# Pooled scores and their products in single PSUM banks in the first eight pairs of an attention and gated-MLP kernel, with a new written-out order

## The chip, the cores and the metric

The kernel runs on one core of one Trainium2 chip. The metric is device time in microseconds (us) for one execution, lower is better. The engines are TensorE (PE; PEld is its weight load), VectorE (DVE), ScalarE (ACT), GpSimd (POOL) and the DMA queues, of which SyncE (SP) issues most.

## The reference

Inputs are q, k, v of shape (8, 8, 576, 64): batch, heads, sequence, head width. Attention has two parts that are added: one over pooled positions (means of four) with full softmax, its rows repeated four times, and a local one in which a position sees only positions less than four away. Its output, heads side by side, goes through a gated MLP.

```python
def sm_attn(qq, kk, vv):
    s = scale * np.matmul(qq, kk.transpose(0, 1, 3, 2))
    a = np.exp(s - np.max(s, axis=-1, keepdims=True))
    return np.matmul(a / (np.sum(a, axis=-1, keepdims=True) + 1e-09), vv)
out_up = np.repeat(sm_attn(q_d, k_d, v_d), 4, axis=2)      # q_d, k_d, v_d: means over groups of 4
scores = np.where(mask, scale * q @ k.T, -1e9)             # mask: |i - j| < 4
x = out_up + softmax(scores) @ v                           # (8, 576, 512)
h = np.maximum(x @ w_in, 0.0)                              # (8, 576, 1024)
u, w = h[..., :512], h[..., 512:]
w_n = (w - mean(w)) / np.sqrt(var(w) + 1e-06)              # over the last axis
w_s = np.einsum('ts,bsd->btd', w_spatial, w_n) + b_spatial[None, :, None]
out = (u * w_s) @ w_out                                    # (8, 576, 512)
```

The host only lays the inputs out; w_in and w_out arrive as 64-bit numbers and are decoded on the chip.

## The kernel before

Work is cut into batches (8), each of four pairs of heads (32 pairs, n = 0 to 31), and each batch then goes through the MLP.

**A pair** (function `attention`). q and k are loaded (qk). Sums over four positions (L720, L723) give the pooled k and q (kd). Local scores S go into a buffer ps by ten windows of 64 positions (L748); where the list ON["mask"] has T, two matmuls ahead of them (L741) add the mask in TensorE, else VectorE adds it (L761). Greatest (L770), difference (L776), exp (L791, or L788 on ScalarE where ON["sub"] has A), sum (L794), reciprocal (L797 and L801 on VectorE, L797 and L799 on GpSimd), division by it (L836), transpose T (L844) with its copy (L846). The pooled scores Sd (L810) make three parts of 144 columns: parts 0 and 2 in a buffer pd, part 1 in a buffer pe. Their greatest (L852 for parts 0 and 2 together, L853 for part 1, L854), exp with sums (L858), reciprocal (L862 with L866 or L864), normalising (L873 on ScalarE, L876 elsewhere), transposes Td (L891, two banks) with copies (L894), and products with the pooled v, AVd (L919, two banks' width), that are moved to dn by ScalarE (L923) and added by VectorE (L926). The local products AV (L952) are added to dn (L971, L973) and split in two f16 parts, x (L1002, L1004).

**A batch's MLP** (function `gated`). Products with the right half of w_in (V, L1029, first batch from 72 us on), their statistics and the split into f16 parts vh (L1038 to L1063), products with the left half (U, L1092), spatial products (SP, L1124), gate (L1145), and output products (O, L1160). The weights are decoded and split ahead of that on VectorE and ScalarE (L513, L539 to L547, L648).

**PSUM** has eight banks. Two double buffers, tag pa (paa, pab: two banks each), and four single ones, tag pm (pma to pmd). A pair from n = 8 on (MERGE = 8) keeps pooled scores and pooled products in the unused ends of the double buffers of local scores and products; in the first eight pairs each has a double buffer of its own. So such a pair takes five pa in turn (ps, pd, pt for T, one for AVd, one for AV) and three pm (pe, two for Td). The MLP's products take one pm each, as do the small products that find scales (L479, L486).

**Order.** The program builds a list of operations with engine, estimated duration and a rank (tables RANK, MRANK, WRANK plus EVICT), and `Plan.run` writes out the order greedily: on each engine, of the operations that could start within NEAR of the first, the lowest rank goes. A buffer is taken when an operation is placed. The lists ON say by index (pair n, or piece of the MLP for vlo) which engine does it; the last letter holds for all further indices. Operations marked port are kept from overlapping between VectorE and GpSimd by the estimate. Up to 110 us the planner fills gaps of TensorE with matmuls that compute nothing (L1204), where a single bank is free by its estimate.

Of the kernel before, what the change touches and what calls it, by code (L numbers as in the profile page):

```python
# [76 lines left out]
class Plan:  # L77
# [61 lines left out]
    def run(self, near=150.0, stay=0.0, dma=(1900.0, 900.0), emit=True):  # L139
# [110 lines left out]

RANK = {"load": [143.005, 47.751, 252.982, -69.47, -172.22, -274.786, 560.411, -758.364, -311.459, 313.434, 266.06, 380.575,
            943.336, 399.915],
        "vload": [391.404, 86.345, 272.249, 337.531, 429.684, -52.69, -370.895, -252.053],
        "vabs": [509.637, -1181.093, -217.316, 87.185, -457.776, 123.004, -794.489, 144.366],
        "tv": [-183.93, 240.18, 765.617, 930.011, 56.071, -19.127, -157.242, 125.859],
        "sum": [-115.268, 142.997, -94.455, -372.167, 362.55, -75.596, 306.456, 702.576, 1696.966, 425.169, -234.075, 705.288,
            -421.357, 223.437],
        "S": [-1061.927, -157.575, 379.809, -830.223, -915.099, 670.631, 141.564, -649.896, 467.386, 88.454, 513.148, 238.256,  # L260
            245.41, 202.772],
        "E": [-534.894, -339.729, -702.236, 21.188, 160.003, 471.872, 219.972, 899.326, -409.142, -823.461, -265.585, -479.069,
            -503.017, -440.633],
        "N": [231.109, -483.572, -754.504, 524.152, -141.085, 397.308, 1325.226, -80.846, -320.013, -220.077, -64.133, -498.673,
            700.859, -253.394],
        "T": [-347.227, -440.539, -1149.413, -139.403, 917.828, -1374.545, -1166.794, 234.909, 536.972, -105.532, -561.257,
            -49.343, -383.904, -24.157],
        "Sd": [-228.884, 341.247, -989.571, 12.731, -290.563, 65.584, -210.501, 584.996, 760.783, -156.288, -493.755, 182.161,
            -206.462, -81.893],
        "Nd": [20.186, -634.328, -625.655, -47.029, -1024.698, 6.919, -369.885, -166.975, -196.395, -51.441, 745.233, 26.68,  # L270
            590.548, 680.939],
        "Td": [226.557, -226.969, 765.057, -163.935, 412.294, -360.224, 842.794, -998.859, 11.321, 28.445, -152.942, 58.045,
            -1153.807, -259.463],
        "AVd": [377.528, -777.682, -319.581, 176.718, 599.105, 1049.442, -339.489, -191.118, -286.676, -150.229, -415.778,
            -182.501, -118.84, 141.634],
        "AV": [60.151, -170.544, -717.724, 720.142, -836.725, 275.504, 440.562, -339.226, -949.724, 57.757, -184.347, -239.42,
            -4.966, -560.047],
        "X": [49.462, -601.369, 382.04, -619.469, -420.239, 803.995, 16.415, -27.426, 201.671, 266.124, -288.114, 118.52,
            -424.608, -87.751]}
MRANK = {"V": [[-120.813, 103.137], [-373.166, -785.223], [-588.287, 86.439], [-457.053, -295.554], [-271.069, 53.075],  # L280
            [-161.929, 7.172], [-384.75, 67.584], [1.753, -86.54]],
        "U0": [[-381.018, 507.475], [-225.844, -398.15], [392.079, 353.99], [415.277, -261.891], [-69.09, -16.703], [-362.251,
            -497.795], [59.314, -190.411], [573.297, -308.684]],
        "S0": [[631.14, 127.639], [-206.013, -184.383], [299.174, 561.899], [-372.357, 30.262], [381.875, 239.103], [33.324,
            19.169], [-136.587, -125.569], [104.744, -531.737]],
        "U1": [[66.951, 205.966], [432.921, 80.243], [202.58, -320.842], [-584.875, -261.385], [85.111, -539.421], [-290.079,
            -515.53], [-73.151, -407.568], [-105.893, -362.577]],
        "O0": [[170.632, -34.982], [-172.469, 696.573], [159.95, -390.053], [-841.668, -359.026], [22.932, -667.87], [-349.956,
            231.605], [321.827, -73.48], [-54.093, -578.395]],
        "S1": [[-122.247, -1002.997], [272.521, 179.124], [-502.627, -34.942], [83.425, -28.324], [193.115, 251.294], [212.725,  # L290
            -514.576], [-0.655, 14.458], [254.101, -410.908]],
        "O1": [[-425.021, 297.386], [239.962, 469.652], [56.568, -208.235], [-194.872, 129.628], [-641.125, -6.104], [281.584,
            274.929], [184.644, 89.516], [19.298, 376.248]]}
EVICT = 456.633
WRANK = {"WV load": [31.22, -21.921, 242.309, 4.474],
        "WV decode": [350.543, -287.444, -567.367, 661.466],
        "WV bound": [-83.736, 162.235, 909.503, 36.755, -835.361],
        "WV split": [-201.598, 11.031, -341.826, -1007.43],
        "WU load": [-364.293, 427.826, 390.089, -59.831],
        "WU decode": [387.574, -316.232, 1019.795, 459.568],  # L300
        "WU bound": [1425.684, -228.293, 245.85, 118.051, 725.352],
        "WU split": [-187.848, -607.313, -258.771, -328.661],
        "WSP load": [289.708, -579.107, 622.627, -316.354, 744.76],
        "WSP bound": [397.382, 106.669, -930.598, 200.751, 873.332, -382.338],
        "WSP split": [-150.625, -91.686, 309.424, 430.824, -1165.74],
        "WO load": [201.774, -325.888, 429.457, 987.307],
        "WO decode": [137.835, 619.019, -225.889, -8.083],
        "WO bound": [-64.148, 457.463, -289.1, 18.247, -58.582],
        "WO split": [620.04, -563.746, 894.059, 1022.164]}
# [20 lines left out]


@with_exitstack
def tile_kernel(ctx, tc, qk, vw, v4, w_in, wT, bsp, w_out, out, emit=True):
# [365 lines left out]
    def attention(n):  # L699
# [550 lines left out]
```

## Time and profile before

| | |
|---|---|
| median of 3 runs | 579.53 us (578.91 to 579.99) |
| profiled execution | 580.97 us, span 579.1 us |
| mean granted TensorE clock | 0.995 of full |
| busy: PE, DVE, ACT, POOL | 551.6, 414.1, 376.3, 186.7 us |

Busy time is a sum over the instructions of an engine without overlap. "Granted clock" is the share of TensorE's full clock. An engine's idle time matters only where work that sets the end waits behind it.

### The profile page before, as it was taken

What the parts mean: (1) busy time and instruction counts of PE and PEld (TensorE: products, weight loads), DVE (VectorE), ACT (ScalarE), POOL (GpSimd) and SP (SyncE); (2) the same over time, 40 slices, a digit from 0 to 9 for tenths busy, and PEclk for the clock granted to TensorE, in tenths of its full rate; (3) what the DMA queues carried; (4) which work ended last, traced back from release to release, by engine and by line L of the source; (5) the groups of instructions that cost most, each with busy time, mean ns of one, the idle gap of its engine ahead of it and who ended that gap; (6) DMA issues with size and microseconds to landing.
All of it is one profiled execution on the core that took longest, in us unless ns stands there. A gap on an engine that the chain in (4) does not pass through costs nothing.

```text
span 579.1 us, 16048 instructions
## 1 busy us (share of the span) xinstructions
PE 551.6 (95%) x6501; PEld 368.0 (64%) x6501; DVE 414.1 (72%) x1084; ACT 376.3 (65%) x1076; POOL 186.7 (32%) x213
## 2 busy tenths in 40 slices
PE   5877899999999998999999999999999999999996
PEld 2445547764786566765776747778567567756752
DVE  5989899964898888578687776781976666844420
ACT  3689999457577677567575877565756665954422
POOL 3636533023531254154330432422422352202100
PEclk9999999999999999999999999999999999999999
DMA  8987870035322344225303343214220400010012
GB/s 285 338 241 213 215 180 1 1 102 143 88 83 91 115 103 126 65 90 138 86 20 119 99 113 102 84 65 108 77 100 2 138 2 19 8 32 1 20 54 74
DMA packets 37390, 57.04 MB, mean 99 GB/s; under 512 B 3650, under 2 KB 24130, under 8 KB 37316
## 3 DMA queue, kind: packets, MB, share of 16 engines
q1 hardware_dynamic: 35012, 48.94, 26.7%
q0 software_dynamic: 2304, 7.08, 7.2%
q8 instruction: 51, 0.84, 0.6%
q14 instruction: 23, 0.19, 0.1%
HBM read 46.57 MB, written 9.44 MB: 97 GB/s over the span
## 4 chain that ended last, share of the span: by engine, by line
PE 70%; DVE 18%; ACT 6%; issue 2%; DMA 2%; POOL 0%; SPq 0%; ACTq 0%; DVEq 0%; POOLq 0%
PE pmd L1124 4%; PE pma L1124 4%; PE pmb L1160 4%; PE pma L1160 4%; PE pmc L1029 4%; PE pmc L1160 4%; PE pma L1029 4%; PE pmc L1124 3%; PE pmb L1124 3%; PE pmd L1029 3%; PE pmd L1092 2%; PE pma L1092 2%; PE pmc L1092 2%; PE pmb L1029 2%; PE pmd L1160 2%
## 5 line engine op out<-in xcount | busy, mean ns | idle before, releaser
L1092 PEld LDWEIGHTS <-win 128*128 128x128 f16 x768 | 74.7, 98 | 20.8 <-issue 0.6
L1124 PEld LDWEIGHTS <-vha 128*128 128x128 f16 x768 | 74.0, 98 | 20.6 <-issue 2.1
L1160 PEld LDWEIGHTS <-gb 128*128 128x128 f16 x264 | 25.6, 98 | 28.5 <-issue 0.4
L1124 PE MATMUL pma<-wsp,vha 128*128 128x256 f16 (+1 forms) x216 | 29.4, 286 | 0.0
L1124 PE MATMUL pmd<-wsp,vha 128*128 128x256 f16 (+1 forms) x204 | 27.6, 285 | 1.3 <-DVE aua L1105 1.3
L1204 PE MATMUL pma<-mask_b,mask_a 128*128 128x512 bf16 x83 | 23.4, 415 | 3.1 <-DVE mask_a L383 3.1
L1124 PE MATMUL pmb<-wsp,vha 128*128 128x256 f16 (+1 forms) x180 | 24.1, 283 | 0.0
L1124 PE MATMUL pmc<-wsp,vha 128*128 128x320 f16 (+1 forms) x168 | 23.5, 290 | 0.0
L1160 PE MATMUL pmb<-wo,gb 128*128 128x512 f16 x96 | 22.0, 379 | 0.0
L1160 PEld LDWEIGHTS <-ga 128*128 128x128 f16 x120 | 11.6, 98 | 12.8 <-issue 0.2
L1057 POOL TENSOR_TENSOR sta<-sta,mhalf 128x1 f32<-128x1 f32 (+1 forms) x14 | 9.0, 646 | 32.3 <-DVE sta L1041 32.3
L669 POOL DMA_DIRECT2D tvb<-v_dram x12 | 10.8, 900 | 18.2 <-DMA tvb<-v_dram 15.7
L1160 PE MATMUL pma<-wo,gb 128*128 128x512 f16 x72 | 16.5, 379 | 0.0
L1029 PEld LDWEIGHTS <-xa 128*128 128x128 f16 x96 | 9.2, 98 | 10.8 <-issue 0.2
L1204 PEld LDWEIGHTS <-mask_a 128*128 128x128 bf16 x85 | 7.9, 104 | 12.6 <-issue 3.7
L720 POOL TENSOR_TENSOR suma<-qka 128x576 f32<-128x576 f32 x6 | 7.8, 1294 | 23.4 <-DMA qka<-qk_dram 23.4
L669 POOL DMA_DIRECT2D tva<-v_dram x12 | 10.8, 902 | 13.2 <-DMA tva<-v_dram 8.9
L1057 POOL TENSOR_TENSOR stb<-stb,mhalf 128x1 f32<-128x1 f32 (+1 forms) x15 | 10.9, 725 | 11.4 <-DVE stb L1041 11.4
L1160 PE MATMUL pmc<-wo,gb 128*128 128x512 f16 x60 | 13.8, 379 | 0.0
L1057 POOL TENSOR_TENSOR stc<-stc,mhalf 128x1 f32<-128x1 f32 (+1 forms) x11 | 7.5, 678 | 18.7 <-DVE stc L1041 15.2
L720 POOL TENSOR_TENSOR sumb<-qkb 128x576 f32<-128x576 f32 x6 | 7.8, 1296 | 16.5 <-DMA qkb<-qk_dram 16.5
L862 POOL TENSOR_SCALAR smdb<-smdb 112x3 f32<-112x3 f32 x3 | 0.6, 201 | 38.6 <-ACT eda L858 38.6
(1085 smaller groups left out, 1725.7 us busy)
## 6 DMA issues: line engine op xcount, KB each, us to landing
qka<-qk_dram SPq DMA_DIRECT2D x15, 576.0 KB, 4.9
qkb<-qk_dram SPq DMA_DIRECT2D x15, 576.0 KB, 6.2
tva<-v_dram POOLq DMA_DIRECT2D x12, 288.0 KB, 5.5
tvb<-v_dram POOLq DMA_DIRECT2D x12, 288.0 KB, 4.3
stg<-w_in_dram SPq DMA_DIRECT2D x5, 512.0 KB, 8.3
out_dram<-rowc SPq DMA_DIRECT2D x7, 256.0 KB, 2.2
out_dram<-rowb SPq DMA_DIRECT2D x7, 256.0 KB, 2.0
out_dram<-rowe SPq DMA_DIRECT2D x7, 256.0 KB, 2.1
```

What stands on the lines that cost most here:

```text
L669: plan.op("POOL", 850, lambda r=r: nc.gpsimd.dma_start(t.ap[LOW:KEYS], v4[b, r], accum_op=ALU.add), w=[t], rank=rank + 2.0 + 0.3 * r, kb=2 ...
L720: side(s1).tensor_tensor(sb.ap.rearrange("p x (g r) -> p x g r", r=2), x[:, :, :, :2], x[:, :, :, 2:], op=ALU.add)
L862: side(ivd).tensor_scalar(smd.ap[:PD], smd.ap[:PD], 1.0e-9, 4.0, op0=ALU.add, op1=ALU.mult)
L1029: nc.tensor.matmul(ps.ap, xs[c].ap[:, i, t * P:(t + 1) * P], win[:, c, j, FF:], start=(c == 0 and (i, j) == (0, 0)), stop=(c == NC - 1 and ...
L1057: plan.op("POOL", 530, lambda: nc.gpsimd.tensor_tensor(st.ap[:r, 8:9], st.ap[:r, 8:9], mhalf[:r], op=ALU.pow), w=[st], rank=rank - EVICT, ...
L1092: nc.tensor.matmul(ps.ap[:, :n], win[:, c, i, ft * P:(ft + 1) * P], xs[c].ap[:, j, HA[h]:HA[h + 1]], start=(c == 0 and (i, j) == (0, 0)), ...
L1124: nc.tensor.matmul(ps.ap[:, :n], vh.ap[:, c, i, fs], wsp[:, c, j, hs], start=(c == 0 and (i, j) == (0, 0)), stop=False)
L1160: nc.tensor.matmul(ps.ap, g.ap[:, c, HA[1] * i + k:HA[1] * i + k + P], wo[:, c, j, :], start=(c == 0 and (i, j) == (0, 0)), stop=(c == NF ...
L1204: nc.tensor.matmul(ap.rearrange("p (j k) -> p j k", k=64), mask_a, mask_b[:, None, :].broadcast_to([P, 8, 64]), start=True, stop=True)
```

## The change

For n < SMALL = 8 the pooled scores' parts 0 and 2 go to two single banks instead of one double buffer, and so do the pooled products (their local products keep a double buffer). A pair then takes three pa and seven pm. The greatest of parts 0 and 2 is found by two reduces instead of one. All ranks, EVICT, NEAR, STAY and the lists ON are new.

```diff
+SMALL = 8
-ON = {"sub": "DDDDDDADDADAAADDDADDAAADDDA",
-        "inv": "DDDDDPDDPDDPDPPDPDPDDPDPDDDPPPPD",
-        "invd": "DDDPDPPDDPDDDDDDPPDDPPDDDDPPPPD",
-        "sum": "DPPPDPPPDDPDPPDDDDPPDPDDDDPDDDPD",
-        "mask": "TTTTTTTTD",
-        "norm": "PDPPPDPDPPDDDPDPPPDPDPDPPPPDDPD",
-        "normd": "PAAPPDPPAAADDPAAPAPADAAPPPPADDAP",
-        "vlo": "PDPDPPPDDPDPDPDDDDPDDPPDDDPDPDDPDPDPDPD"}
+ON = {"sub": "DDDDDDADDADDDDADAAAAAADDAAAAAAD",
+        "inv": "DDDDDDDDDPDDDDDDDDPDPDPPPPDPPPD",
+        "invd": "DDDPDDPPDPDPDDDDPDDDDPPPPDPPPDP",
+        "sum": "DPPPDPDPDDDDPDPPPPDDPDDPPDDDDDP",
+        "mask": "TTTTTTTDTD",
+        "norm": "PDPDDDPPPPDPDPDPDDDPDDDPDPDDDDDP",
+        "normd": "PAAAPADADDAAAPDPPDAPDADPDAPDDDAD",
+        "vlo": "DDPDPDDDPPPPDDDPDPDDDDDPDDPDPD"}
...
-        merge = n >= MERGE
+        merge, small = n >= MERGE, n < SMALL
...
         def third(e):
-            return pe.ap[:, :G] if e == 1 else pd.ap[:, 256 * e + at:256 * e + at + G]
+            if e == 1:
+                return pe.ap[:, :G]
+            return pd[e // 2].ap[:, :G] if small else pd.ap[:, 256 * e + at:256 * e + at + G]
...
-            pd = plan.buf("pa")
+            pd = (plan.buf("pm"), plan.buf("pm")) if small else plan.buf("pa")
...
         def maximum_d():
-            nc.vector.tensor_reduce(mxd.ap[:PD, ::2], pd.ap[:PD].rearrange("p (e k) -> p e k", e=2)[:, :, at:at + G], axis=AX.X, op=ALU.max, negate=True)
+            if small:
+                for e in (0, 2):
+                    nc.vector.tensor_reduce(mxd.ap[:PD, e:e + 1], third(e)[:PD], axis=AX.X, op=ALU.max, negate=True)
+            else:
+                nc.vector.tensor_reduce(mxd.ap[:PD, ::2], pd.ap[:PD].rearrange("p (e k) -> p e k", e=2)[:, :, at:at + G], axis=AX.X, op=ALU.max, negate=True)
...
+        pdl = pdt if small else (pdt,)
         if not merge:
-            plan.op("PE", 610, scores_d, r=[kb], w=[pd, pe], hold=[ed], rank=R["Sd"], lag=PEL, mode="Q", name="Sd")
-        plan.op("DVE", 780, maximum_d, r=[pdt, pe], w=[mxd], rank=R["Sd"] - EVICT, port=True, name="maxd")
+            plan.op("PE", 610, scores_d, r=[kb], w=[*pdl, pe], hold=[ed], rank=R["Sd"], lag=PEL, mode="Q", name="Sd")
+        plan.op("DVE", 840 if small else 780, maximum_d, r=[*pdl, pe], w=[mxd], rank=R["Sd"] - EVICT, port=True, name="maxd")
...
-        if up:
+        if small:
+            two_w, two_v = (plan.buf("pm"), plan.buf("pm")), (plan.buf("pa"),)
+        elif up:
```

## Rows read from the trace of the kernel before

**Rows 1.** Busy time of each engine by stretch (microseconds from the start of the span; first the length of the stretch, then each engine's busy time with its number of instructions, the granted clock of TensorE, the share of DMA time and GB/s), and the sum over the whole span.
```profile
14.50:72.40 57.90, 46.31 (x775) 28.27 (x773) 52.44 (x134) 48.78 (x142) 31.10 (x33) 0.98 0.88 252
72.40:116.00 43.60, 41.88 (x339) 28.29 (x338) 42.11 (x119) 34.39 (x84) 11.04 (x12) 1.00 0.25 60
116.00:565.00 449.00, 446.26 (x5251) 303.54 (x5250) 310.89 (x814) 285.26 (x840) 139.52 (x149) 1.00 0.27 77
sum 579.10, PE 551.61 PEld 367.99 DVE 414.05 ACT 376.32 POOL 186.68; mean PE 110.32 PEld 73.60 DVE 82.81 ACT 75.26 POOL 37.34
```

**Rows 2.** The same table for the filler matmuls (line L1204) alone, opening stretch.
```profile
14.50:72.40 57.90, 18.55 (x70) 5.92 (x68) 0.98 0.88 252
```

**Rows 3.** The same table for all instructions, the last two quarters of the opening.
```profile
43.50:58.00 14.50, 11.34 (x243) 7.57 (x241) 14.30 (x34) 13.94 (x41) 9.16 (x10) 1.00 0.73 212
58.00:72.40 14.40, 11.92 (x241) 7.95 (x241) 12.75 (x39) 14.02 (x41) 8.47 (x9) 1.00 0.87 215
```

**Rows 4.** Waits of VectorE from 14.5 to 72.4 us: what waited, the releaser, microseconds in total, times, the longest.
```profile
DVE mxb L770 <- PE pab L748: 1.6, 1, 1.6
DVE mxc L770 <- PE paa L748: 0.6, 1, 0.6
DVE xfb L971 <- issue: 0.4, 1, 0.4
```

**Rows 5.** Waits of TensorE's matmuls in the same stretch, columns as in rows 4.
```profile
PE paa L952 <- ACT eda L858: 1.3, 1, 1.3
PE pab L952 <- ACT eda L858: 1.3, 1, 1.3
PE pab L741 <- DVE dnb L926: 1.2, 1, 1.2
PE paa L741 <- DVE sma L794: 0.9, 1, 0.9
PE paa L810 <- ACT edb L858: 0.6, 1, 0.6
```

**Rows 6.** From the timeline: VectorE and ScalarE instructions whose durations serve as prices (start, duration, engine, line, operation, output and inputs, count; in brackets the idle time before it and its releaser).
```profile
10.46 0.46 DVE L723 TENSOR_TENSOR kda<-suma 128x288 f32<-128x288 f32 x1
16.64 0.46 DVE L852 TENSOR_REDUCE mxda<-paa 112x2 f32<-112x288 f32 x1 [0.56 <-PE paa L810]
17.02 0.30 DVE L853 TENSOR_REDUCE mxda<-pmb 112x1 f32<-112x144 f32 x1
22.48 0.22 DVE L801 RECIPROCAL smb<-smb 128x10 f32<-128x10 f32 x1
24.06 0.81 DVE L836 TENSOR_TENSOR sb<-sb,smb 128x640 f32<-128x640 f32 x1
33.06 1.03 ACT L873 ACTIVATE eda<-eda,smdc 112x144 f32<-112x144 f32 x3 [0.51 <-DVE smdc L866]
```

**Rows 7.** From the timeline: matmuls and the ScalarE reads that end the use of the buffers with pooled scores of pair 0 (paa) and pair 7 (paa with pmc), in order of time.
```profile
17.36 0.47 PE L810 MATMUL pab<-kdb 64*64 64x144 f32 x8
18.79 0.38 ACT L858 ACTIVATE eda<-paa,mxda 112x144 f32<-112x144 f32 x1
19.31 0.43 PE L741 MATMUL paa<-mask_b,mask_a 128*128 128x320 bf16 x2 [0.90 <-DVE sma L794]
72.42 0.82 PE L1029 MATMUL pmb<-win,xa 128*128 128x512 f16 x3
75.02 0.81 PE L1029 MATMUL pma<-win,xa 128*128 128x512 f16 x3
76.17 0.38 ACT L858 ACTIVATE edb<-paa,mxdd 112x144 f32<-112x144 f32 x1
```

**Rows 8.** Four lines of code by instruction: count, duration in ns as least, median and greatest, first and last start in microseconds, shape.
```profile
L720 DVE TENSOR_TENSOR suma<-qka x9: 739/751/2402, 9.7 to 409.3; 128x576 f32<-128x576 f32 x9
L797 DVE TENSOR_SCALAR sma<-sma x5: 145/164/1020, 25.6 to 503.4; 128x10 f32<-128x10 f32 x5
L854 DVE TENSOR_SCALAR mxda<-mxda x8: 170/170/1173, 17.4 to 455.2; 112x3 f32<-112x3 f32 x8
L542 DVE TENSOR_SCALAR mba<-rowa x2: 428/956/1484, 6.5 to 50.4; 128x512 int32<-128x512 int32 x2
```

**Rows 9.** From the timeline: GpSimd instructions of the opening, columns as in rows 6.
```profile
27.45 1.14 POOL L720 TENSOR_TENSOR sumb<-qkb 128x576 f32<-128x576 f32 x1
43.91 0.91 POOL L876 TENSOR_TENSOR edb<-edb,smdd 112x432 f32<-112x432 f32 x1
44.78 1.26 POOL L836 TENSOR_TENSOR sa<-sa,smd 128x640 f32<-128x640 f32 x1
49.77 1.79 POOL L836 TENSOR_TENSOR sb<-sb,smb 128x640 f32<-128x640 f32 x1 [0.51 <-DVE smb L801]
55.84 0.89 POOL L864 TENSOR_TENSOR smda<-smda,minus 112x3 f32<-112x3 f32 x1
56.71 1.14 POOL L720 TENSOR_TENSOR suma<-qka 128x576 f32<-128x576 f32 x1
57.92 0.92 POOL L723 TENSOR_TENSOR kda<-suma 128x288 f32<-128x288 f32 x1
64.22 0.91 POOL L876 TENSOR_TENSOR eda<-eda,smdc 112x432 f32<-112x432 f32 x1
65.90 1.98 POOL L799 TENSOR_TENSOR smc<-smc,minus 128x10 f32<-128x10 f32 x1
```

More of the change, by code (lines that the diff above doesn't have):

```diff
@@ L247, in run @@
         return end
[L253 to L309, printed above, removed]
@@ L310 @@
-NEAR = 104.496
-STAY = 26.882
+RANK = {"load": [264.533, 33.649, 403.06, 186.653, -42.381, -410.839, 819.039, -607.622, -501.728, 243.085, 352.102, 354.132,
+            1093.505, 273.573],
+        "vload": [558.967, 276.5, 334.545, 308.567, 267.188, -101.291, -379.396, -222.862],
+        "vabs": [634.178, -1182.863, -145.804, -180.742, -589.109, 166.874, -730.049, 207.057],
+        "tv": [-43.519, 464.187, 742.381, 810.054, 111.484, -44.852, -198.988, 180.839],
+        "sum": [-322.043, 168.123, 112.107, -348.8, 434.587, 59.773, 244.669, 938.335, 1550.758, 527.842, -255.301, 697.748,
+            -232.674, 238.406],
+        "S": [-1302.427, 29.544, 240.133, -921.679, -943.4, 626.644, -32.63, -685.185, 661.359, 184.729, 567.017, 361.726,
+            321.012, 376.66],
+        "E": [-459.669, -527.995, -658.247, 159.782, 193.317, 620.643, 306.329, 873.564, -326.981, -885.141, -348.277, -551.906,
+            -474.543, -373.478],
+        "N": [285.362, -589.13, -711.842, 524.689, -161.908, 293.474, 1265.404, -30.543, -412.846, -159.808, -52.343, -537.504,
+            815.595, -307.896],
+        "T": [127.389, -609.648, -1127.039, -425.66, 749.486, -1310.231, -1100.363, 438.252, 691.047, -87.719, -528.186, -24.871,
+            -375.456, -91.404],
+        "Sd": [-347.5, 377.51, -1003.842, -215.136, -365.115, 138.976, -92.298, 652.174, 329.267, -160.095, -401.819, 232.758,
+            -236.92, -140.505],
+        "Nd": [238.956, -699.96, -990.36, -323.516, -1004.45, -222.865, -239.071, 39.976, -46.443, -133.498, 796.176, 63.19,
+            573.005, 754.815],
+        "Td": [354.384, -309.784, 945.407, -253.79, 312.905, -196.204, 736.782, -793.133, -122.62, 50.663, -245.263, 4.127,
+            -993.967, -317.459],
+        "AVd": [537.656, -772.178, -275.255, 18.365, 579.22, 945.875, -136.534, -217.582, -170.692, -264.39, -400.831, -116.318,
+            -79.309, -14.534],
+        "AV": [58.38, 226.865, -858.713, 622.045, -1014.049, 531.897, 160.75, -457.568, -982.583, 5.951, -166.95, -376.233,
+            -23.789, -699.464],
+        "X": [84.426, -678.614, 198.865, -615.758, -322.875, 1205.879, 53.938, -269.106, 245.79, 341.802, -225.41, 243.327,
+            -310.041, -131.769]}
@@ new lines @@
+MRANK = {"V": [[-357.918, 142.233], [-583.398, -902.948], [-392.849, 65.793], [-486.121, -186.54], [-280.761, 71.703], [-130.958,
+            80.968], [-507.617, 17.881], [65.81, -197.574]],
+        "U0": [[-349.34, 320.11], [66.062, -306.805], [332.204, 335.878], [316.833, -270.829], [-105.368, -214.951], [-323.961,
+            -452.914], [36.997, -107.838], [626.35, -336.686]],
+        "S0": [[493.25, -41.501], [-259.464, -183.334], [281.386, 638.165], [-394.019, 42.503], [488.16, 84.052], [92.242,
+            95.678], [-89.856, -104.179], [126.907, -592.501]],
+        "U1": [[12.184, 237.505], [257.792, -21.302], [159.007, -287.556], [-621.089, -364.793], [143.193, -392.905], [-338.506,
+            -488.257], [-13.595, -342.975], [-108.576, -404.447]],
+        "O0": [[225.164, 130.003], [-178.642, 778.718], [87.794, -329.345], [-911.542, -274.843], [133.598, -636.006], [-412.8,
+            235.349], [471.326, -78.114], [-117.512, -536.116]],
+        "S1": [[-2.809, -401.391], [302.578, 113.58], [-558.903, 129.581], [129.33, -158.619], [319.352, 256.614], [164.414,
+            -533.905], [-70.901, 129.294], [234.596, -407.925]],
+        "O1": [[-467.107, 369.251], [188.194, 415.668], [-56.45, -278.037], [-170.601, 91.132], [-852.743, 37.137], [186.673,
+            294.551], [295.701, 77.537], [10.665, 429.525]]}
@@ new lines @@
+EVICT = 412.459
+WRANK = {"WV load": [117.529, -191.416, 536.853, -123.356],
+        "WV decode": [381.441, -309.174, -504.673, 989.236],
+        "WV bound": [-96.239, 347.932, 921.213, 220.458, -744.06],
+        "WV split": [-41.433, 205.029, -31.901, -1111.787],
+        "WU load": [-505.686, 267.048, 436.293, -55.911],
+        "WU decode": [590.144, -496.64, 1133.635, 346.647],
+        "WU bound": [1437.453, -178.104, 204.387, 241.312, 794.104],
+        "WU split": [-340.217, -481.128, -248.193, -257.007],
+        "WSP load": [412.862, -748.696, 636.427, -698.741, 707.973],
+        "WSP bound": [338.999, 65.666, -1274.432, 344.193, 1131.126, -377.36],
+        "WSP split": [20.858, -150.513, 67.002, 283.654, -1096.433],
+        "WO load": [106.864, -276.43, 554.521, 1285.607],
+        "WO decode": [269.914, 593.385, -262.761, 151.235],
+        "WO bound": [15.036, 477.917, -226.203, 173.049, -153.32],
+        "WO split": [731.701, -664.422, 905.427, 931.649]}
@@ L313 @@
+NEAR = 106.678
+STAY = 29.333
 WARM = 110000.0
@@ L876, in normal_d @@
                 side(nd).tensor_tensor(t, t, smd.ap[:PD, :, None, None].broadcast_to([PD, 3, 2, KEYS - LOW]), op=ALU.mult)
+        pdl = pdt if small else (pdt,)
         if not merge:
-            plan.op("PE", 610, scores_d, r=[kb], w=[pd, pe], hold=[ed], rank=R["Sd"], lag=PEL, mode="Q", name="Sd")
-        plan.op("DVE", 780, maximum_d, r=[pdt, pe], w=[mxd], rank=R["Sd"] - EVICT, port=True, name="maxd")
-        plan.op("ACT", 1120, exp_d, r=[pdt, pe, mxd], w=[ed, smd], rank=R["Sd"] - EVICT, name="expd")
+            plan.op("PE", 610, scores_d, r=[kb], w=[*pdl, pe], hold=[ed], rank=R["Sd"], lag=PEL, mode="Q", name="Sd")
+        plan.op("DVE", 840 if small else 780, maximum_d, r=[*pdl, pe], w=[mxd], rank=R["Sd"] - EVICT, port=True, name="maxd")
+        plan.op("ACT", 1120, exp_d, r=[*pdl, pe, mxd], w=[ed, smd], rank=R["Sd"] - EVICT, name="expd")
         ivd = Way("invd", n, P=("POOL", 1400, True), D=("DVE", 300, True))
```

## Prediction

> **What bounds the kernel now.** The table of stretches comes first [rows 1]. TensorE is busy for 551.61 us of the 579.10 us span, so only the rest, 27.5 us, can be idle time. By stretch that is 11.6 us from 14.5 to 72.4 us, 1.7 us from 72.4 to 116 us, 2.7 us from 116 to 565 us and, by difference, 11.5 us before the first and behind the last of these times. The busy time also holds filler matmuls that compute nothing; from 14.5 to 72.4 us they take 18.55 us [rows 2]. So of the 57.9 us of that stretch TensorE spends 30.1 us on nothing and 27.8 us on work. From 116 us on it is the bound, and nothing but its own work counts. The first matmul of the wide products (L1029) stands at 72.42 us [rows 7]. What this change can win lies ahead of it and just behind it.
>
> The reader is next to see that TensorE doesn't set the pace there. VectorE is busy for 52.44 of the 57.9 us and for 42.11 of the 43.6 us after them, ScalarE for 13.94 of 14.5 us and 14.02 of 14.4 us in the two last quarters of the opening [rows 1, 3]. So from 14.5 to 116 us VectorE idles for 5.46 + 1.49 = 6.95 us, 1.56 us of it for a load at the very start [rows 4]. That leaves 5.39 us.
>
> The list of TensorE's waits in the opening shows where double-bank buffers are the cause [rows 5]. Five waits end with the instruction that frees a double buffer which held pooled scores or their product with v, or for which such scores stood in line: the values (L952) wait twice for exp of pooled scores (L858), the pooled scores (L810) once for the same, the masks of new scores (L741) for L926 and once for exp (the row names L794, but the last read of the same buffer paa, L858, ended at 19.17 us, just ahead of the 19.31 us at which L741 starts [rows 7]). The sum is 1.3 + 1.3 + 1.2 + 0.9 + 0.6 = 5.3 us.
>
> **The change, part by part.** Per pair, five double buffers and three single banks become three and seven. The five waits lose their cause: 5.3 us of TensorE time at most. But TensorE has 30.1 us to spare, so they count only where VectorE starves behind them. It does so twice: 0.6 us (L770 behind L748) and 0.4 us (L971 behind the values, "issue") [rows 4]. The floor of the gain is 0, if another wait takes the place, the direct gain 1.0 us, and the ceiling all 5.39 us of VectorE's idle time. That idle time is the currency of the rest.
>
> The greatest of the pooled scores: one reduce of 2 x 144 columns becomes two of 144. A reduce of 288 lasts 0.46 us and one of 144 0.30 us [rows 6]. By durations that is +0.14 us, times eight pairs +1.1 us. Neighbours overlap by 0.08 us (L852 starts at 16.64 and ends at 17.10, L853 starts at 17.02 [rows 6]); with that taken from the added one it is +0.06 us, times eight +0.5 us. I take 0.9 us, between the two. The matmuls, the three exps and the two moves of the products are as many as before, on other addresses: nothing.
>
> The lists that share out work move more than the buffers do. Ahead of 72.4 us VectorE takes over the sums of pair 6 (0.75 + 0.46 = 1.21 us), the division by the sums of pairs 3 and 4 (2 x 0.81), two reciprocals with their additions in pair 5 (0.16 + 0.22, and the pooled one priced alike: 0.77 in all); the pooled normalising of pair 5 leaves it and that of pair 6 comes: nothing [rows 6, 8]. With the 0.9 us that is +4.5 us. GpSimd loses 1.14 + 0.92 + 1.26 + 1.79 + 1.98 + 0.89 + 2 x 0.91 = 9.8 us [rows 9]. This pays back: some VectorE instructions last far longer than the usual, such as the 2.40 us of L720 instead of 0.75 us, while GpSimd ran the same operation (27.45 us) [rows 8, 9]. The four great cases, each less its median (for L542 its least), cost 1.65 + 0.86 + 1.00 + 1.06 = 4.6 us beside 31.10 us of GpSimd work [rows 1, 8], or 0.15 us for one. So 9.8 us less should give back 1.4 us; the bounds are 0 and 4.6 us. VectorE's net is +3.1 us.
>
> The Trainium skill (SBUF — State Buffer, Who interferes with whom) says that VectorE and GpSimd share a port pair as an exclusive lock and that the loser is blocked for the whole instruction, in the forms that need the pair. The 2.40 us row agrees in kind; taken for each removed GpSimd instruction the rule would give back 9.8 us instead of 1.4 us, more than the 4.6 us that these rows hold.
>
> From 72.4 to 116 us VectorE gets one more low-part subtraction of the first batch and an added mask in pair 7 (each at most the 0.81 us of L836), and loses that pair's division (0.81) and pooled reciprocal (0.39): +0.4 us. ScalarE gets the pooled normalising of pairs 3 and 5, 1.03 us each by the copies of L873 [rows 6]. In the last two quarters it has 14.5 - 13.94 + 14.4 - 14.02 = 0.9 us free [rows 3], so this is covered only if deferrable ScalarE work moves behind 72.4 us.
>
> Sum on VectorE: of 5.39 us of idle time 3.1 + 0.4 = 3.5 us is used up, and 1.9 us is the most that the first 116 us can shrink while the amount of work stands. I take 1.6 us: most of it, because the new order can place its instructions without the five waits, not all, because the one direct figure is 1.0 us. The queues of loads aren't changed in kind; ranks move them, at no price that I can read. After 116 us nothing changes but order, under a TensorE with 2.7 us of idle time in 449 us.
>
> The profiled execution took 580.97 us with its span of 579.1 us; the median of the runs is 579.53 us, 1.44 us lower. So the profile should read about 579.4 us and the median 577.9 us. About 0.2%, 1.2 us, is what a measurement can tell here.
>
> **Rivals.** (a) GpSimd's relief is the greater one: all 4.6 us go instead of 1.4 us. The gain is 1.6 + 3.2 = 4.8 us: 574.7 us. For it speaks that GpSimd loses a third of its opening; against it that most instructions beside it are undisturbed.
>
> (b) Slower: single banks run out. A pair's pooled scores now take three of the four single banks at once, from L810 until the last exp. Two such pairs can't overlap any more: pair 1's scores came at 17.36 us, while pair 0's were read until 19.17 us, so 1.8 us later [rows 7]. And pair 7's, held until 76.55 us, leave one bank to the wide products that start at 72.42 us: the second of them, at 75.02 us, would wait 1.5 us [rows 7]. If both come through, +3.3 us less the direct 1.0 us is +2.3 us: 581.8 us. It decides from the point where a Td (two banks) or a wide product stands in the queue behind a pair's three banks. Against it: the order may put such work elsewhere.
>
> (c) Slower: ScalarE becomes the bound before 72.4 us. 2.1 us more against 0.9 us free is +1.2 us: 580.7 us. It decides where none of its work is deferred.
>
> (d) The opening gets shorter and gives it back: the wide products start earlier, but VectorE, 97% busy from 72.4 to 116 us [rows 1], can't feed them, and TensorE idles behind it. No change: 579.5 us. This also holds if the banks are freed and nothing was waiting for them but fillers.
>
> **How the numbers follow.** The forecast has 0.36, (a) 0.12, (b) 0.18, (c) 0.10, (d) 0.24. Faster is the forecast and (a), 0.48; same is (d), 0.24; slower is (b) and (c), 0.28. The forecast's own range is 577.6 to 578.5 us (1.0 to 1.9 us of gain). For 8 in 10 the range must reach both signs: low 574.5 us, at (a), and high 582.0 us, past (b), whose waits may be repeated in later pairs (what is left out).
>
> **What would show it.** In the profile after: fewer fillers and waits of L741, L952 and L919 on L858, L926 and L973 before the first L1029; this matmul at 70 to 71 us; VectorE's idle time from 14.5 to 116 us at about 3.5 us or less and its busy time some 3 us greater; no VectorE row above 2 us. Wrong if L1029 or L891 now waits for L858 or L926 (b), if ScalarE shows no gap ahead of an L1029 that comes later (c), if L1029 comes earlier and idle time from 72.4 to 116 us grows by as much (d), or if the granted clock of the opening falls because no single bank is free for fillers; with 30.1 us to spare that costs little unless it lasts past 72.4 us.

## The result: 5.5 us slower, and the profile after

The changed kernel takes 585.15 us (median of 4 runs, 584.92 to 586.66) beside 579.70 us for the kernel before on the same chip: a ratio of 1.0102 (95% interval 1.0082 to 1.0122). The forecast was 577.9 us, the range 574.5 to 582.0 us. Sign and range were both missed.

The profiled execution of the changed kernel took 586.66 us with a span of 584.9 us, 5.8 us more than the span of before. In its code the fillers stand in line L1215, the masks of new scores in L743, scores S in L750, pooled scores Sd in L814, their exp in L866, Td in L900, the pooled products AVd in L930, the local products AV in L963, the wide products V in L1040.

The table of stretches in the form of [rows 1], in the first two rows with the same limits as there, then with the limits moved to the first wide product, which now stands at 77.30 us instead of 72.42 us [rows 7]; the last row is the filler line alone [rows 2].

```profile
14.50:72.40 57.90, 43.71 (x614) 27.04 (x618) 51.26 (x136) 46.70 (x138) 19.28 (x24) 0.85 0.84 247
116.00:565.00 449.00, 445.77 (x5267) 305.80 (x5265) 315.92 (x837) 279.72 (x829) 138.23 (x144) 1.00 0.27 76
14.50:77.30 62.80, 47.66 (x704) 30.03 (x704) 56.05 (x152) 50.45 (x147) 19.99 (x24) 0.86 0.84 242
77.30:120.90 43.60, 41.80 (x341) 28.51 (x339) 39.90 (x107) 35.61 (x88) 10.16 (x11) 1.00 0.20 45
14.50:72.40 57.90, 15.79 (x58) 5.41 (x58) 0.85 0.84 247
```

In the 43.6 us from the first wide product on TensorE does what it did before (41.80 us of work beside 41.88 [rows 1]). The first wide product comes 4.88 us later, and that is 4.88 of the 5.8 us; the other 0.9 us stand behind it. By VectorE's ledger up to that point: it is busy for 56.05 us instead of 52.44 us, +3.6 us, and idle for 62.80 - 56.05 = 6.75 us instead of 5.46 us, +1.3 us. Behind it VectorE is busy for 39.90 us instead of 42.11 us, with 107 instructions instead of 119: the new order also puts work ahead of the first wide product that stood behind it before. GpSimd lost 31.10 - 19.28 = 11.8 us of the opening, and the granted clock of that stretch is 0.85 instead of 0.98.

Waits of TensorE's matmuls over the whole span (columns as in [rows 5]).

```profile
PE pma L481 <- ACT junk L650: 5.1, 1, 5.1
PE pmb L900 <- POOL eda L884: 2.1, 1, 2.1
PE pmb L814 <- ACT pdTa L903: 1.6, 1, 1.6
PE pmb L814 <- DVE dna L937: 1.2, 1, 1.2
PE pmb L814 <- ACT eda L866: 1.1, 1, 1.1
PE pma L930 <- ACT eda L866: 0.9, 1, 0.9
PE pmd L814 <- ACT pdTa L903: 0.9, 1, 0.9
```

The five waits of [rows 5] are gone, as the prediction said. In their place the pooled scores and products wait for single banks: 1.6 + 1.2 + 1.1 + 0.9 + 0.9 = 5.7 us beside the 5.3 us removed. The first row is the longest: the product that finds a scale of w_in's left half (L481, named WU below) stands at the head of TensorE's queue for 5.1 us.

The table of stretches from 60 to 74 us in steps of 2 us (the column of the granted clock is the third from the end), and TensorE's timeline around that wait and at the first wide product.

```profile
60.00:62.00 2.00, 2.00 (x55) 1.38 (x54) 1.97 (x6) 2.00 (x7) 0.00 (x0) 1.00 0.95 328
62.00:64.00 2.00, 0.29 (x3) 0.09 (x1) 1.86 (x12) 1.84 (x11) 0.00 (x0) 1.00 0.96 328
64.00:66.00 2.00, 0.00 (x0) 0.00 (x0) 1.19 (x3) 2.00 (x10) 0.37 (x2) 0.74 1.13 285
66.00:68.00 2.00, 0.56 (x9) 0.34 (x13) 1.85 (x3) 1.97 (x5) 1.58 (x2) 0.50 0.30 63
68.00:70.00 2.00, 2.00 (x44) 1.89 (x41) 0.88 (x4) 1.94 (x6) 0.00 (x0) 0.50 0.82 129
70.00:72.00 2.00, 2.00 (x55) 1.67 (x57) 0.95 (x7) 1.41 (x3) 0.93 (x1) 0.55 0.13 27
72.00:74.00 2.00, 2.00 (x60) 1.63 (x52) 2.00 (x6) 0.45 (x2) 1.11 (x2) 1.00 0.57 117
```

```profile
62.12 0.17 PE L488 MATMUL pma<-sxa,ones_b 4*128 4x1 bf16 x1
67.44 0.38 PE L481 MATMUL pma<-ident,sw 128*4 128x128 f32 x1 [5.15 <-ACT junk L650]
67.75 1.54 PE L963 MATMUL pab<-probTa,vc 64*64 64x60 f32 x40
72.19 0.86 PE L963 MATMUL paa<-probTb,vd 64*64 64x60 f32 x40
77.30 0.82 PE L1040 MATMUL pmb<-win,xa 128*128 128x512 f16 x3
```

TensorE does nothing from 62.3 to 67.4 us, the granted clock falls from 1.00 (2.4 GHz) to 0.50 (1.2 GHz), and the same local products last 1.54 us at 67.75 us and 0.86 us at 72.19 us. VectorE, which needs these results, is busy for 0.88 and 0.95 of 2 us meanwhile. Two more stretches of the opening have a low clock, 0.50 from 28 to 34 us and 0.59 from 54 to 58 us:

```profile
28.00:34.00 6.00, 4.43 (x24) 3.23 (x24) 4.68 (x12) 4.24 (x14) 1.35 (x2) 0.50 1.00 257
54.00:58.00 4.00, 3.81 (x19) 1.51 (x23) 3.93 (x11) 3.04 (x11) 0.00 (x0) 0.59 0.60 185
```

So there were four suspects: the scarce single banks, the clock, one blocked VectorE instruction (below), and the place of that scale product in the queue.

### The profile page after: what moved, and what is told of

It reads as the page before. It is cut to its first block, busy times and chain, and to the rows that moved or that the text cites. A ratio compares the mean times of both kernels' runs of the same rounds, so it can differ in the third digit from the quotient of the medians.

```text
span 584.9 us, 16060 instructions
## 1 busy us (share of the span) xinstructions
PE 554.6 (95%) x6491; PEld 372.3 (64%) x6491; DVE 418.5 (72%) x1107; ACT 374.5 (64%) x1073; POOL 174.4 (30%) x199
## 4 chain that ended last, share of the span: by engine, by line
PE 73%; DVE 11%; ACT 10%; DMA 3%; issue 1%; SPq 1%; POOL 0%; ACTq 0%; DVEq 0%
PE pma L1135 4%; PE pmd L1171 4%; PE pmb L1135 4%; PE pmc L1040 4%; PE pmc L1135 3%; PE pmb L1103 3%; PE pmd L1135 3%; PE pma L1103 3%; PE pma L1040 3%; PE pmd L1040 3%; PE pmd L1103 3%; PE pmb L1171 3%; PE pma L1171 3%; PE pmc L1171 3%; PE pmb L1040 3%; PE pmc L1103 3%
## 5 line engine op out<-in xcount | busy, mean ns | idle before, releaser
L1135 PE MATMUL pma<-wsp,vha 128*128 128x256 f16 (+1 forms) x240 | 32.1, 283 | 0.0
L1135 PE MATMUL pmb<-wsp,vha 128*128 128x320 f16 (+1 forms) x180 | 24.7, 287 | 1.0 <-DVE aua L1116 0.9
L1135 PE MATMUL pmd<-wsp,vha 128*128 128x256 f16 (+1 forms) x180 | 24.4, 285 | 0.0
L1171 PE MATMUL pmd<-wo,gb 128*128 128x512 f16 x96 | 22.0, 379 | 0.0
L1068 POOL TENSOR_TENSOR stb<-stb,mhalf 128x1 f32<-128x1 f32 (+1 forms) x14 | 9.2, 657 | 41.5 <-DVE stb L1052 39.5
L1215 PE MATMUL pma<-mask_b,mask_a 128*128 128x512 bf16 x55 | 15.1, 424 | 3.1 <-DVE mask_a L385 3.1
L1040 PEld LDWEIGHTS <-xa 128*128 128x128 f16 x96 | 9.3, 98 | 11.3 <-issue 0.8
L1068 POOL TENSOR_TENSOR sta<-sta,mhalf 128x1 f32<-128x1 f32 (+1 forms) x15 | 11.0, 734 | 18.3 <-DVE sta L1052 18.2
L1068 POOL TENSOR_TENSOR stc<-stc,mhalf 128x1 f32<-128x1 f32 (+1 forms) x11 | 9.1, 823 | 24.8 <-DVE stc L1052 24.8
L1215 PEld LDWEIGHTS <-mask_a 128*128 128x128 bf16 x75 | 7.5, 107 | 12.7 <-issue 4.3
L870 POOL TENSOR_SCALAR smdb<-smdb 112x3 f32<-112x3 f32 x4 | 2.4, 596 | 39.9 <-ACT edb L866 38.4
L1171 PE MATMUL pma<-wo,gb 128*128 128x512 f16 x60 | 13.8, 379 | 0.0
```

The lines of the kernel that those rows point to most:

```text
L870: side(ivd).tensor_scalar(smd.ap[:PD], smd.ap[:PD], 1.0e-9, 4.0, op0=ALU.add, op1=ALU.mult)
L1040: nc.tensor.matmul(ps.ap, xs[c].ap[:, i, t * P:(t + 1) * P], win[:, c, j, FF:], start=(c == 0 and (i, j) == (0, 0)), stop=(c == NC - 1 and ...
L1068: plan.op("POOL", 530, lambda: nc.gpsimd.tensor_tensor(st.ap[:r, 8:9], st.ap[:r, 8:9], mhalf[:r], op=ALU.pow), w=[st], rank=rank - EVICT, ...
L1135: nc.tensor.matmul(ps.ap[:, :n], vh.ap[:, c, i, fs], wsp[:, c, j, hs], start=(c == 0 and (i, j) == (0, 0)), stop=False)
L1171: nc.tensor.matmul(ps.ap, g.ap[:, c, HA[1] * i + k:HA[1] * i + k + P], wo[:, c, j, :], start=(c == 0 and (i, j) == (0, 0)), stop=(c == NF ...
L1215: nc.tensor.matmul(ap.rearrange("p (j k) -> p j k", k=64), mask_a, mask_b[:, None, :].broadcast_to([P, 8, 64]), start=True, stop=True)
```

## The experiments

**Single banks with the order of before.** The written-out order and the lists of the kernel before are kept operation by operation; an operation stands back only where no buffer is free. Three kernels: both buffers single, the scores alone, the products alone. The first two parts of this edit are in all three. The third makes the scores alone single and the fourth the products alone; each is given beside the kernel with both.

```diff
-            for eng, ops in todo.items():
...
-            _, t, o = best
+        queue = [self.ops[i] for i in self.order]
+        while queue:
+            for pos, o in enumerate(queue[:600]):
+                if o.wait:
...
-            two_w, two_v = (plan.buf("pm"), plan.buf("pm")), (plan.buf("pa"),)
+            two_w, two_v = [(plan.buf("pa"),) for _ in range(2)]
...
-        merge, small = n >= MERGE, n < SMALL
+        merge, small = n >= MERGE, False
```

Both: 

> The old lists and the old order of operations, written out one by one, with only the buffers changed: in the first eight pairs pooled scores and pooled products in single banks. An operation stands later than in the old order only where it would find no bank free. Theory 'banks': the single banks themselves cost the time, since three of four are taken at once; then this is at 583 to 588 us, with new waits of pooled scores, pooled products or transposes on L-lines that free single banks, and the first wide product (L1040 here, L1029 before) several us after 72.4 us. Theory 'order': the loss comes with the new order and lists alone; then this stays at 578 to 581 us.

Measured: 592.69 us, ratio 1.0211 (1.0182 to 1.0240), with the signs of theory 'banks' but above its range; the first wide product at 81.60 us. The two longest waits of TensorE:

```profile
PE pmb L1085 <- ACT edb L911: 3.9, 1, 3.9
PE pmb L975 <- ACT edb L911: 3.3, 1, 3.3
```

Here L1085 is the first wide product and L911 the exp of pooled scores. It is the place that rival (b) named, though (b) had the second wide product wait and not the first, and the price is twice and more what (b) gave it.

Scores alone: 

> The old lists and the old order, with only the pooled scores of the first eight pairs in single banks (their products stay in a double buffer). With both in single banks this order took 592.7 us. Theory 'three of four': the cost comes from the pooled scores, which hold three single banks until the last exp; then this is at 586 to 591 us, and waits for L-lines of the exp stand before the pooled products or the first wide products. Theory 'too many users': each of the two moves costs about half, 584 to 588 us.

Measured: 586.75 us, ratio 1.0119 (1.0089 to 1.0149), inside both ranges. The timeline shows the wide product behind the last read of pair 7's third part:

```profile
76.98 0.38 ACT L911 ACTIVATE edb<-pmb,mxdd 112x144 f32<-112x144 f32 x1
77.14 0.95 PE L1085 MATMUL pma<-win,xa 128*128 128x512 f16 x3 [3.95 <-ACT edb L911]
```

Products alone: 

> The old lists and the old order, with only the pooled products in single banks. Theory 'three of four': 580 to 582 us, since two banks held for a short copy are found at most places. Theory 'too many users': 584 to 588 us.

Measured: 582.38 us, ratio 1.0047 (1.0033 to 1.0060), 0.4 us above the range of 'three of four' and 1.6 us below the other. The first wide product comes at 72.21 us, as early as before, and the clock of the opening is 1.00; the loss stands behind it:

```profile
72.21:115.81 43.60, 40.25 (x322) 26.75 (x321) 39.89 (x110) 33.46 (x83) 11.04 (x12) 1.00 0.26 62
```

TensorE does 40.25 us of work there instead of 41.88 us [rows 1]. What follows from the three: in the old order single banks cost 13 us, some 7 us with the scores alone and 2.9 us with the products alone; most of it is the scores. The lists and the new order win back 592.69 - 585.15 = 7.5 us of that, not all.

**The new order with double buffers.**

```diff
-SMALL = 8
+SMALL = 0
```

The written-out order of the changed kernel is kept by the same code as above.

> The lists and the written-out order of the changed kernel, operation by operation, with the double buffers of the kernel before (one reduce of two parts again); an operation stands back only where no buffer is free. Theory of the banks (an order is made for its buffers, neither is good alone): five double buffers a pair must now go where three went, so 590 us or more. Rival (the new lists and ranks are slower by themselves, whatever the buffers): between 583 and 588 us. If the new order is sound and the single banks alone are bad, it is 581 us or less.

Measured: 593.46 us, ratio 1.0239 (1.0222 to 1.0256), the first wide product at 80.28 us. An order and its buffers belong together: either crossing of the two costs 13 to 14 us beside the kernel before. This says nothing on which pair is the better one. No run keeps an order in this way with its own buffers, so what keeping it costs by itself isn't shown; the products alone, whose first wide product came as early as before, show that it is little up to there.

**The second reduce alone**, in the kernel before.

```diff
-            nc.vector.tensor_reduce(mxd.ap[:PD, ::2], pd.ap[:PD].rearrange("p (e k) -> p e k", e=2)[:, :, at:at + G], axis=AX.X, op=ALU.max, negate=True)
+            if merge:
...
+            else:
+                for e in (0, 2):
+                    nc.vector.tensor_reduce(mxd.ap[:PD, e:e + 1], third(e)[:PD], axis=AX.X, op=ALU.max, negate=True)
```

> The kernel before with the greatest of the pooled scores found by two reduces of 144 columns instead of one of 288 in the first eight pairs, nothing else touched. By the prediction's price (0.06 to 0.14 us for each pair on a VectorE that is busy for 97%) it is slower by 0.5 to 1.1 us: 580.0 to 580.6 us. Rival: they go into VectorE's idle time and nothing can be measured: within 0.3 us of the kernel before.

Measured: 580.14 us beside 579.55 us, ratio 1.0013 (1.0002 to 1.0025): +0.6 us of median, with 0.1 to 1.4 us in the interval. The price of 0.9 us in the prediction's sum lies inside it, and so does the rival's 0.3 us.

**The blocked VectorE instruction.** In the changed kernel one reciprocal step on 112x3 numbers lasts 3.52 us, while GpSimd runs three operations one behind the other (the timeline):

```profile
22.98 0.15 DVE L870 TENSOR_SCALAR smda<-smda 112x3 f32<-112x3 f32 x1
24.39 3.52 DVE L870 TENSOR_SCALAR smdb<-smdb 112x3 f32<-112x3 f32 x1 [0.73 <-ACT edb L866]
24.38 1.43 POOL L722 TENSOR_TENSOR sumb<-qkb 128x576 f32<-128x576 f32 x1
25.49 1.18 POOL L884 TENSOR_TENSOR eda<-eda,smda 112x432 f32<-112x432 f32 x1
26.35 1.52 POOL L840 TENSOR_TENSOR sa<-sa,sma 128x640 f32<-128x640 f32 x1
```

The instruction is left out for pair 1, whose pooled part then comes out four times too large.

```diff
-            side(ivd).tensor_scalar(smd.ap[:PD], smd.ap[:PD], 1.0e-9, 4.0, op0=ALU.add, op1=ALU.mult)
+            if n != 1:
+                side(ivd).tensor_scalar(smd.ap[:PD], smd.ap[:PD], 1.0e-9, 4.0, op0=ALU.add, op1=ALU.mult)
```

> The changed kernel without one VectorE instruction: the addition and multiplication ahead of the reciprocal in pair 1's pooled part, which lasted 3.52 us at 24.39 us while GpSimd ran three instructions back to back (that pair's pooled part comes out four times too large). Theory 'block': ScalarE and VectorE ran 2 us behind from there on and nothing made it good; then the first wide product comes about 2.3 us earlier and the time is 582 to 583.5 us. Theory 'order': another wait takes its place, and the time is 584.5 to 585.5 us.

Measured: 585.52 us, ratio 1.0107 (1.0086 to 1.0129), no better than the changed kernel's 1.0102. VectorE now waits for ScalarE instead, and ScalarE for a load:

```profile
DVE mbf L544 <- ACT rowa L541: 2.3, 1, 2.3
ACT rowa L541 <- DMA stg<-w_in_dram: 2.0, 1, 2.0
```

So 2.3 us of the block are time that this load takes anyway. This suspect falls.

**The scale product moved** behind the local products of pairs 2 and 3 in the written-out order; the two VectorE steps that read its result move with it, and nothing else (the edit of the order, by the names of its operations).

```diff
-bound(WU), AV(2), T(3), S(5), AVd(3), AV(3)
+AV(2), T(3), S(5), AVd(3), AV(3), bound(WU)
```

> The changed kernel with one operation moved: the product that turns the sums for the scale of w_in's left half, at which TensorE stood idle for 5.1 us (62.3 to 67.4 us), now stands behind the local products of pairs 2 and 3. Theory 'queue': the work behind it (L963, L848, L750, L930) was ready and only stood in line; then the wait vanishes, the granted clock doesn't fall at 65 us, the first wide product comes at 74.5 to 76 us instead of 77.3 us and the time is 582.5 to 584.5 us. Theory 'order': the work behind it waits for xb's second part at 67 us anyway, or the left half of w_in comes later by as much; 584.5 to 586 us.

Measured: 587.75 us (585.59 to 589.87), ratio 1.0130 (1.0092 to 1.0168), above both ranges. The 5.1 us wait is gone and another has come:

```profile
PE pab L795 <- DVE xfb L1029: 3.9, 1, 3.9
```

L795 is the next scores, behind the addition to x of a pair that is late itself. So the place in the queue isn't the cause: TensorE's inputs are late there, whoever stands first.

**Fillers by hand.** To hold the clock, matmuls that compute nothing are put ahead of instructions that wait, into the banks that these own already.

```diff
         def turn_b():
+            if fill:
+                plan.warm(pb.ap, fill)
...
         def turn_d():
+            if n == 0:
+                plan.warm(ptd[0].ap, 9)
...
+            if n in (2, 5):
+                plan.warm(pd[0].ap, 7 if n == 2 else 6)
```

In turn_b, which issues a scale product, fill is 22 at that of w_out (WO) in the first kernel, not at the one that waits: 44 fillers in all.

> The changed kernel with 44 more filler matmuls, put ahead of the four places where TensorE stands idle before the first wide product (the transposes of pair 0, the pooled scores of pairs 2 and 5, and the product for the scale of w_out that waits 5.1 us). Theory 'clock': the granted clock of 0.5 from 28 to 34, 55 to 58 and 65 to 72 us costs what the change lost; then the clock of the opening is back near 1.00, the first wide product comes at 73 to 75 us and the time falls from 585.2 to 580 to 583 us. Theory 'order': only the slow stretch on the chain from 67.4 to 71.6 us counts, about 1 us, and the time is 584 to 585 us.

Measured: 589.37 us, ratio 1.0166 (1.0144 to 1.0189). The 22 fillers fell where TensorE had no gap:

```profile
87.74 4.92 PE L1221 MATMUL pmd<-mask_b,mask_a 128*128 128x512 bf16 x22
```

They last 4.92 us and the time grew by 589.37 - 585.15 = 4.2 us. Not all of it is theirs: in the profiled execution, 3.8 us longer by its span (588.7 us), the first wide product comes 1.05 us later, and 2.75 us are added behind it, where the 22 fillers stand.

```profile
78.35 0.82 PE L1046 MATMUL pmb<-win,xa 128*128 128x512 f16 x3
```

The time lies above both ranges. As a test of the clock this kernel misses its aim. Together with the change of pair 1:

> Both edits together (the pooled part of pair 1 is again four times too large). Theories 'clock' and 'block', each with its own share: the gains add up, 3 to 5 us, to 580 to 582 us. Theory 'order': 583.5 to 585 us.

Measured: 588.94 us, ratio 1.0164 (1.0143 to 1.0184): the same, and again above both ranges.

The second has fill=23 at WU, where the 5.1 us wait is, 45 in all:

> The changed kernel with 45 more fillers, 23 of them now at the wait of 5.1 us itself (the earlier run had put them at another product for a scale, at 87.7 us, where TensorE had no gap, and there 4.9 us of fillers made the time 4.2 us longer). Theory 'clock': the products from 67.4 to 71.6 us run at full clock, about 2 us shorter, the first wide product comes at 75 to 76 us and the time is 582.5 to 584.5 us. Theory 'queue': the clock is a by-product and the wait stays: 584.5 to 586 us.

Measured: 584.60 us (582.09 to 586.80, 6 runs), ratio 1.0088 (1.0058 to 1.0118). Its profiled execution, in the stretches up to the first wide product and behind it:

```profile
14.50:74.00 59.50, 51.38 (x749) 30.74 (x747) 54.66 (x152) 50.04 (x147) 20.17 (x24) 1.00 0.88 257
74.00:117.60 43.60, 41.78 (x341) 28.53 (x339) 39.89 (x107) 35.63 (x88) 10.16 (x11) 1.00 0.19 43
```

The clock is 1.00 throughout and the first wide product comes at 74.00 us, 3.3 us earlier than in the changed kernel; the wait of the scale product is filled. A VectorE block as long as the one above stands in this execution too, at another instruction, and the first wide product comes earlier all the same:

```profile
24.51 3.75 DVE L724 TENSOR_TENSOR suma<-qka 128x576 f32<-128x576 f32 x1
```

The six executions don't agree, and each lists its mean clock:

| mean granted clock | 1.000 | 0.998 | 1.000 | 0.997 | 0.995 | 0.994 |
|---|---|---|---|---|---|---|
| time, us | 582.09 | 582.98 | 583.62 | 585.59 | 586.18 | 586.80 |

With one exception, the lower the clock, the longer the time; which of the two brings the other is not shown by this table alone. The three fastest are 1.5 to 3.1 us faster than the changed kernel's median, but the median of all six is only 0.55 us faster, and the intervals of the two ratios overlap. Even the fastest is 2.6 us slower than the median of before that was taken beside it (579.49 us).

**More fillers**, 41 on top of these, ahead of the pooled scores and transposes of nearly every pair.

```diff
-            if n in (2, 5):
-                plan.warm(pd[0].ap, 7 if n == 2 else 6)
+            if small and n:
+                plan.warm(pd[0].ap, {2: 7, 5: 6}.get(n, 4))
...
-            if n == 0:
-                plan.warm(ptd[0].ap, 9)
+            if small:
+                plan.warm(ptd[0].ap, 3 if n else 9)
```

> The changed kernel with the fillers of the run fillers_wu and 41 more (four ahead of the pooled scores of the pairs 1, 3, 4, 6 and 7, three ahead of the transposes of the pooled scores of the pairs 1 to 7), some 8.7 us more at the 0.21 us of one. Clock theory (the times of fillers_wu, 582.1 to 586.8 us, differ because the clock held in some executions only): the mean clock is 0.998 or more in every execution and all times are 581.5 to 583.5 us. Rival (the fillers stand in the path themselves, since TensorE waits in this kernel where the banks come free late): the clock holds too, but the time is 584 us or more in every execution.

Measured: 586.71 us (585.68 to 588.55), ratio 1.0128 (1.0106 to 1.0150), clock 0.996 to 0.999.

```profile
14.50:77.11 62.61, 57.19 (x790) 33.46 (x783) 54.35 (x152) 50.78 (x147) 20.73 (x24) 1.00 0.87 247
```

The clock holds and the first wide product is as late as in the changed kernel: TensorE is now busy for 57.19 of 62.61 us, and the fillers stand in the path. The rival's sentence came true.

**The clock by itself**: the kernel before without its fillers from 14.5 to 72.4 us.

```diff
-                if self.warm and t < WARM:
+                if self.warm and (t < COLD or 72000.0 < t < WARM):
```

> The kernel before with its fillers from 14.5 to 72.4 us left out (18.55 us of them in its profile), nothing else touched: what the clock alone is worth in the opening. Clock theory (about half of the loss of the changed kernel is its clock, which stands at half speed in several stretches of the opening): without the fillers the opening's mean granted clock falls to 0.85 or less, the first wide product comes 2 to 4 us after 72.4 us and the time is 582 to 584 us. Rival (what the prediction said: with 30 us of TensorE to spare a lower clock costs little unless it lasts past 72.4 us): the clock falls as far, but the first wide product stays within 0.5 us and the time at 579 to 580 us.

Measured: 585.07 us (584.90 to 585.56) beside 579.55 us, ratio 1.0097 (1.0082 to 1.0113), more than even the clock theory said. Nothing but matmuls that compute nothing was taken out, and the kernel lost 5.5 us. By the traces every engine has the same other instructions in the same order as before; only which of the single banks some of them use is changed.

```profile
14.50:76.75 62.25, 39.53 (x694) 30.50 (x694) 50.92 (x132) 49.20 (x141) 29.49 (x32) 0.70 0.85 235
76.75:120.35 43.60, 41.88 (x339) 28.29 (x338) 42.11 (x119) 34.34 (x84) 10.20 (x11) 1.00 0.24 58
```

The clock of the opening is 0.70 instead of 0.98. TensorE still has 62.25 - 39.53 = 22.7 us of idle time there. Yet VectorE idles for 62.25 - 50.92 = 11.3 us instead of 5.5 us [rows 1], and the first wide product comes 4.3 us later. It is a chain in which each engine waits for the other, so slower matmuls lengthen it though TensorE has room on average.

The Trainium skill (TensorE: Matmul & The Clock Gate, HAM oscillation — how this bites in real kernels) puts the penalty of throttled matmul time at half of it. Taken for all of this stretch that is at half speed, 62.25 x (0.30 / 0.50) = 37 us, that would be an estimate of some 19 us. By the rows TensorE, which idles for over a third of the stretch, spends 39.53 us on its work instead of 46.31 - 18.55 = 27.76 us [rows 1, 2], 11.8 us more, and 5.5 us of that reach the end: the page's figure is a ceiling here.

## Why the prediction was wrong

**The five waits lose their cause: right, and worth nothing.** They are gone, and 5.7 us of new waits for single banks stand in their place. (The direct gain of 1.0 us was read from two waits of VectorE; the same list has a third of the kind, 0.6 us of L971 behind L952.) The floor of 0 in the prediction's bounds is what came of it; "another wait takes the place" was written down and not carried into the sum.

**VectorE's work: about right ahead of the wide products, wrong behind.** The sum said +3.1 us up to the wide products. Measured is +3.6 us in the changed kernel and +2.2 us (54.66 - 52.44) where the clock held. Behind the first of them it said +0.4 us, and 2.2 us less was measured in both: the sum went by the lists and didn't see that the order moves work forward, to where it is paid. The second reduce, 0.9 us in the sum, measured 0.6 us.

**The relief by less GpSimd work, 1.4 us: not seen.** GpSimd lost 11.8 us of the opening, 2 us more than the sum had, and a block longer than any in [rows 8] came, 3.52 us beside three operations in a row. With a second one it makes up for all that was gone: less the usual duration of their lines, the two cost 3.4 + 1.4 = 4.8 us beside the 4.6 us of the four cases before.

```profile
51.14 1.85 DVE L544 TENSOR_SCALAR mbc<-rowe 128x512 int32<-128x512 int32 x1
```

Rival (a) falls with it. The Trainium skill's rule (SBUF — State Buffer, Who interferes with whom) that the loser of the port pair is shut out agrees with the row of 3.52 us: it ends at 27.91 us, the third GpSimd operation at 27.87 us. That fewer GpSimd instructions must free time in proportion was my own step.

**The step that failed: VectorE's idle time as "the currency of the rest".** The sum let 3.5 us of new work go into 5.39 us of idle time and took 1.6 us of the rest as the gain. But that idle time is no store. It is made by inputs that come late, and new work doesn't move them. Up to the end of the 43.6 us behind the first wide product, where the prediction wanted it to fall from 6.95 us to about 3.5 us, it grew to 6.75 + 3.70 = 10.45 us. Even with the clock held it shrank by 0.6 us only ahead of the first wide product (59.50 - 54.66 = 4.84 us beside 5.46 us), while the work grew by 2.2 us: +1.6 us at the first wide product, where the prediction had -1.6 us.

**The second failing step: "with 30.1 us to spare [a lower clock] costs little unless it lasts past 72.4 us".** The run without fillers refutes it: 5.5 us for a clock of 0.70 that is back at 1.00 before the first wide product. The loss of clock in that stretch is 62.25 x 0.30 = 18.7 us against 57.9 x 0.02 = 1.2 us before, so one us of lost clock costs 5.5 / 17.5 = 0.31 us there. The changed kernel loses 62.8 x 0.14 = 8.8 us; 7.6 us more than before at 0.31 is 2.4 us, an estimate, for the rate isn't a constant: between the fastest and the slowest execution with fillers at the long wait the lost clock differs by 0.006 x 585 = 3.5 us and the time by 4.7 us. That run gives 1.5 to 3.1 us by its three fastest executions and 3.3 us by the first wide product of the fastest, but 0.55 us by its median. So 2 to 3 us of the 5.5 us may be the clock. The split isn't shown, and the rest, VectorE's work, the new waits and the order, I haven't taken apart further.

**Rival (b), single banks run out: the right mechanism, mis-sized.** It was given 0.18 and +2.3 us. Its two places came up as named: pair 1's scores behind pair 0's exp cost 1.1 us in the changed kernel (1.8 us in the forecast), and the first wide product behind pair 7's exp 3.9 us in the old order (1.5 us for the second in the forecast; the new order avoids it). What it lacked was repetition through the pairs and the half clock behind the gaps: with the old order it is 13 us. Rival (d) doesn't apply, since the opening got longer. Rival (c) fails by its sign, for ScalarE's idle time up to the first wide product grew from 9.1 to 12.35 us. But from 60 to 70 us ScalarE is busy for 9.75 of 10 us, and the longest wait of TensorE ends with one of its sums (L650): in that stretch it does set the pace. No run gave its added work back, so what that costs stays open.

## What to carry to other kernels

Removing named waits can be worth nothing until the waits that the new resource will cause are counted the same way: here three of four single banks a pair, held from the scores to the last exp. In a stretch where several engines feed each other in turn, the idle time of the busiest one isn't free room, and matmuls that compute nothing can be the cheapest part of a schedule, provided that they stand in real gaps. Compare a new buffer layout together with an order made for it, and try the crossings as well, since these show how much of a result is order and how much buffers.

## What the runs showed of the hardware

In a gap of 5.1 us on TensorE its granted clock fell from 1.00 to 0.50, and it stayed near there through some 4 us of nearly unbroken matmuls (68 to 72 us), which I hadn't expected to matter in a stretch with spare TensorE time. The same program held its clock in some executions and not in others (0.994 to 1.000 in six runs, 582.1 to 586.8 us). Kernels with such gaps may be less steady: this one spread over 4.7 us and the one with the scale product moved over 4.3 us in four runs, the kernel before over 1.9 us in 13 runs and 3.5 us in 15 others. One VectorE instruction on 112x3 numbers took 3.52 us instead of 0.15 us through three GpSimd operations in a row; without it the time was no shorter.
